# A new order for the opening's list of steps in a fused attention and feed-forward kernel

## Chip, core and metric

The kernel runs on one core of a Trainium2 chip. The metric is the time of one execution on the device, in microseconds (us). The engines of the core work side by side: TensorE (PE in the profile, its weight loads PEld), VectorE (DVE), ScalarE (ACT), GpSimd (POOL) and SyncE (SP). GpSimd and SyncE also issue transfers between the chip's memory and the core's on-chip memory; one queue belongs to each.

## What is computed

Sliding-window causal attention (window 64, sequence 576, 8 batches of 8 heads of 64), whose output feeds a two-layer block with the activation h * cos(h):

```python
scores = (1 / sqrt(D)) * q @ k.T                  # per batch and head
mask = (rel >= 0) & (rel < 64)                    # rel = query position - key position
attn = softmax(where(mask, scores, -1e9))
x = (attn @ v) as (8 * 576, 8 * 64)               # 4608 tokens of 512
h = x @ w_in                                      # 512 -> 2048
out = (h * cos(h)) @ w_out                        # 2048 -> 512
```

Inputs and output are float32; the kernel works on bfloat16 copies of them.

## The kernel before

The 4608 tokens go in nine blocks of 512 (mt = 0 to 8). For each block the attention output of the tokens must stand transposed in a tile xT; TensorE then forms h in 16 slices of 128 features (h_ps), ScalarE takes the sine of h plus a quarter turn (that is the cosine), VectorE multiplies both (gT), and TensorE forms the output from gT and w_out.

Attention works on groups of up to four units (a pair of heads and 64 query rows each). A group goes through scores (TensorE), row maximum (VectorE), exponential with its row sum (ScalarE), reciprocal of the sum (VectorE), normalisation (a multiply, GpSimd or VectorE), transposition of the weights (TensorE and a copy, or a transposing transfer of SyncE), and the product with v (TensorE).

Within each engine instructions run in the order of the program text, so that order is the schedule. From block 1 on a planner with due times interleaves attention of a later batch with the feed-forward of the current block. For the opening, which is block 0's attention and feed-forward and block 1's attention, the order is written out by hand in the string FIRST: 300 steps, separated by blanks. A step is a name and its arguments, separated by points; a last letter d, a, p or s gives the engine (VectorE, ScalarE, GpSimd, a transfer of SyncE), a last digit of s, Gs, h and o the PSUM bank (0 to 4 for O1, X0, X1, S, O0). The names:

- Lq, Lk, Lv, Lwi, Lwo: loads of q, k, v and of quarters of w_in and w_out (first argument of Lq, Lk, Lv: the batch). All are issued by GpSimd, except Lq0.0 and Lk0.0 by SyncE, which cq and ck then cast. io, mk, mc: the masks.
- tq, tk, Tq, Tk: transpositions of a pair of heads of batch 0 and 1 on TensorE (line 202), and pq, pk, Pq, Pk: the copies out of PSUM (lines 123, 224, 226).
- s, m, e, i, n, w, c with pair and half: scores (lines 306, 313), maximum (323), exponential (340), reciprocal (350), normalisation (357), transposition (373) and its copy (123) for a group of batch 0. Gs, Gm, Ge, Gi, Gn, Gw or Gc, Gp with a number: the same for groups 8 to 18. Gc of groups 9 to 14 is a transposing transfer of SyncE (376). In Gm (line 328) the masked scores go into one of six tiles.
- zA, zB, zC, yA, yB, y: copies that lay out v once more, shifted by 64 rows (spread_v).
- v and V: products with v for block 0 and 1 (lines 410, 392); x and X: copies of their output into xT.
- h, S, g: half a block's h product (line 424), its sine (430) and the gate product (436). tb and tb2 load the sine's and the exponential's table.
- o: a quarter of the second product for 128 tokens (line 443); oc: its copy out.

Three PSUM buffers (tag "t", pool ps_t) serve all transpositions and most attention outputs:

```python
ps_t = ctx.enter_context(tc.tile_pool(name="ps_t", bufs=3, space=PSUM))
t_ps = ps_t.tile([128, S], BF16, tag="t", name=f"t{name}_ps")
s = att.tile([128, GF, 128], F32, tag="s", name="s", bufs=6)
```

The second of these is in transposed(), the third in g_max(). A new tile waits until the last reader of the buffer that it takes is done.

Of the kernel before, what the change touches and what calls it, by code (L numbers as in the profile page):

```python
# [10 lines left out]
def _safe_warn(msg, *a, **kw):  # L11
# [31 lines left out]


FIRST = (
# [18 lines left out]
)  # L64


# [670 lines left out]
```

## Time and profile before

| | |
|---|---|
| median of 3 runs | 304.21 us (302.83 to 304.63) |
| profiled execution, its own time | 303.25 us |
| its span, first to last instruction | 301.5 us |
| TensorE busy | 291.7 us (97%) |
| VectorE, ScalarE, GpSimd busy | 233.9, 232.1, 209.1 us |
| packets of GpSimd's transfer queue | 100192, 18.06 MB |
| granted TensorE clock | 1.0 |

Times in the profile count from the start of the span. A timeline row has start, duration, engine, line, operation, tiles (out<-in), shapes and count, and in brackets the idle time of the engine before it and what ended that. A row of the groups has a count, the time busy and the mean duration in nanoseconds, then the idle time ahead. A row of the transfers ends with the median time from issue to landing. A row of the chain of work that ended last has start, duration and what.

### The profile page before, as it was taken

How to read it: one execution, taken by the hardware profiler on the slowest of the kernel's cores; microseconds unless marked ns; L12 is line 12 of the kernel's file. 1: busy time of each engine (PE TensorE's matmuls, PEld its weight loads, DVE VectorE, ACT ScalarE, POOL GpSimd, SP SyncE). 2: the span in 40 equal slices, each digit the busy share in tenths (PEclk: the TensorE clock that was granted, in tenths of full speed). 3: DMA queues.
4: the chain of work that ended last, by engine and by line, in shares of the span. 5: the costliest groups of instructions: out<-in, count | busy, mean ns of one | idle time of the engine just before them, and what ended most of it. 6: DMA issues, size and time to landing. Idle time of an engine off the chain costs nothing.

```text
span 301.5 us, 8520 instructions
## 1 busy us (share of the span) xinstructions
PE 291.7 (97%) x2936; PEld 163.8 (54%) x2936; DVE 233.9 (78%) x915; ACT 232.1 (77%) x781; POOL 209.1 (69%) x238
## 2 busy tenths in 40 slices
PE   3989999999999999999999999999999999999996
PEld 2768854644455445444454445445544454785485
DVE  3798887898887886788678865887588658985794
ACT  5899699877987699769986998699978997304610
POOL 8899568996999689986998799878995860000000
PEclk9999999999999999999999999999999999999999
DMA  7999999999999994999999999999699944003013
GB/s 144 176 205 194 197 188 143 96 139 175 222 116 99 234 143 94 100 149 199 181 106 150 186 159 121 128 196 176 120 97 133 203 88 157 0 3 141 1 35 107
DMA packets 158732, 41.47 MB, mean 138 GB/s; under 512 B 146976, under 2 KB 154336, under 8 KB 158688
## 3 DMA queue, kind: packets, MB, share of 16 engines
q0 software_dynamic: 100192, 18.06, 84.0%
q1 hardware_dynamic: 58352, 22.79, 40.8%
q8 instruction: 23, 0.38, 0.5%
q14 instruction: 21, 0.17, 0.2%
q10 hardware_dynamic: 144, 0.07, 0.1%
HBM read 36.70 MB, written 9.44 MB: 153 GB/s over the span
## 4 chain that ended last, share of the span: by engine, by line
PE 80%; DMA 10%; ACT 6%; POOL 1%; issue 1%; DVE 0%; POOLq 0%; SPq 0%
PE h_ps L460 37%; PE out_ps L697 23%; PE out_ps L547 8%; DMA w_out<-in_moe_w_out_dram 6%; ACT e L340 5%; PE out_ps L443 3%; PE o_ps L392 3%; PE s_ps L291 2%; DMA wT<-w 2%; DMA k<-in_k_dram 2%; PE tq_ps L205 1%; PE s_ps L313 1%; POOL w L357 1%; PE s_ps L306 0%; ACT kT L123 0%
## 5 line engine op out<-in xcount | busy, mean ns | idle before, releaser
L460 PE MATMUL h_ps<-xT,w_in 128*128 128x512 bf16 x512 | 115.1, 379 | 0.2
L686 DVE TENSOR_TENSOR gT<-h_ps,sin 128x512 bf16<-128x512 f32 x128 | 85.2, 688 | 25.8 <-ACT sin L683 25.2
L683 ACT ACTIVATE sin<-h_ps 128x512 f32<-128x512 f32 x128 | 73.8, 598 | 37.3 <-PE h_ps L460 37.0
L340 ACT ACTIVATE e<-s,negm 128x128 f32<-128x128 f32 (+1 forms) x256 | 97.1, 381 | 2.0 <-DVE negm L328 1.0
L697 PE MATMUL out_ps<-w_out,gT 128*128 128x512 bf16 x384 | 85.3, 379 | 0.0
L357 POOL TENSOR_TENSOR w<-e,rden 128x512 bf16<-128x512 f32 (+1 forms) x68 | 69.1, 1034 | 17.0 <-DVE rden L350 12.6
L460 PEld LDWEIGHTS <-w_in 128*128 128x128 bf16 x512 | 48.9, 98 | 54.4
L697 PEld LDWEIGHTS <-gT 128*128 128x128 bf16 x384 | 36.5, 98 | 43.1
L328 DVE CUSTOM_DVE_ANT_0 s<-s_ps,mask 128x128 f32<-128x128 f32 (+1 forms) x256 | 56.0, 277 | 2.0 <-PE s_ps L313 1.7
L340 ACT ACTIVATION_READ_ACCUMULATOR e<-s,negm 128x1 f32 x256 | 48.0, 188 | 0.0
L168 POOL DMA_DIRECT2D q<-in_q_dram x36 | 28.6, 794 | 13.5 <-DMA v<-in_v_dram 5.3
L174 POOL DMA_DIRECT2D v<-in_v_dram x40 | 34.2, 869 | 1.1 <-DMA q<-in_q_dram 1.1
L168 POOL DMA_DIRECT2D k<-in_k_dram x36 | 28.5, 792 | 1.3 <-DVE gT L686 0.6
L350 DVE RECIPROCAL rden<-den 128x4 f32<-128x4 f32 (+1 forms) x73 | 12.2, 167 | 18.8 <-ACT e L340 18.5
L123 POOL COPY v<-v 64x1536 bf16<-64x1536 bf16 (+3 forms) x16 | 22.9, 1433 | 0.4
L328 DVE DVE_READ_ACCUMULATOR2_ANT negm<- 128x1 f32 x256 | 21.3, 83 | 0.0
L123 DVE CAST xT<-o_ps 128x512 bf16<-128x512 f32 x24 | 15.6, 680 | 4.9 <-PE o_ps L392 4.7
L443 PE MATMUL out_ps<-w_out,gT 128*128 128x512 bf16 x64 | 14.8, 379 | 0.2 <-DMA w_out<-in_moe_w_out_dram 0.2
L424 PE MATMUL h_ps<-xT,w_in 128*128 128x256 bf16 x128 | 14.7, 273 | 0.0
L547 PEld LDWEIGHTS <-sums 128*128 128x128 bf16 x136 | 12.2, 98 | 2.0 <-DVE sums L492 0.4
L424 PEld LDWEIGHTS <-w_in 128*128 128x128 bf16 x128 | 12.3, 98 | 1.4
L123 ACT CAST xT<-o_ps 128x512 bf16<-128x512 f32 x12 | 7.1, 612 | 6.4 <-PE o_ps L392 6.4
(85 smaller groups left out, 312.4 us busy)
## 6 DMA issues: line engine op xcount, KB each, us to landing
out_dram<-out_sb SPq DMA_DIRECT2D x16, 512.0 KB, 7.7
v<-in_v_dram POOLq DMA_DIRECT2D x32, 128.0 KB, 6.0
q<-in_q_dram POOLq DMA_DIRECT2D x36, 96.0 KB, 8.6
k<-in_k_dram POOLq DMA_DIRECT2D x36, 96.0 KB, 9.0
w_in<-in_moe_w_in_dram POOLq DMA_DIRECT2D x4, 512.0 KB, 9.0
w_out<-in_moe_w_out_dram POOLq DMA_DIRECT2D x4, 512.0 KB, 11.3
q<-in_q_dram POOLq DMA_DIRECT2D x7, 144.0 KB, 6.3
k<-in_k_dram POOLq DMA_DIRECT2D x7, 144.0 KB, 6.2
```

Of the source, the lines that this page charges most:

```text
L123: {"a": nc.scalar.copy, "p": nc.gpsimd.tensor_copy}.get(engine, nc.vector.tensor_copy)(out, in_)
L168: nc.gpsimd.dma_start(out=st[name, b][:, c].rearrange("p (h d) -> p h d", h=H), in_=src.rearrange("h p d -> p h d"))
L174: nc.gpsimd.dma_start(out=vt.rearrange("p (h d) -> p h d", h=H), in_=v[b, :, c * 128:c * 128 + n, :].rearrange("h p d -> p h d"))
L328: nc.vector.tensor_tensor_reduce(out=s[:, u, c], in0=s_ps[:, u, c], in1=mask[:, 2 - j % 2 if j else 0, c], scale=-scale if b else -1.0, sc ...
L340: nc.scalar.activation(e[:, u, c], s[:, u, c], AF.Exp, bias=negm[:, u:u + 1], scale=1.0 if n < n_first else -1.0, accum_out=den[:, u:u + 1])
L357: (nc.gpsimd if engine == "p" else nc.vector).tensor_tensor(out=w[:, 0:u], in0=e[:, 0:u], op=ALU.mult, in1=rden[:, 0:u].unsqueeze(2).to_br ...
L424: nc.tensor.matmul(out=h_ps[:, half * e:half * e + half], lhsT=w_in_sb[:, ks, ff * 128:ff * 128 + 128], rhs=st["xT", 0][:, ks, half * g:ha ...
L460: nc.tensor.matmul(out=st["h", ff], lhsT=w_in_sb[:, ks, ff * 128:ff * 128 + 128], rhs=st["xT", mt][:, ks], start=start, stop=stop)
L547: nc.tensor.matmul(out=to[n_] if split else to[:, e], lhsT=lhs[name][f // 2][:, f % 2, 128 * e:128 * e + 128], rhs=rhs[name][:, f, lo:hi], ...
L683: nc.scalar.activation(sin, h_ps, AF.Sin, bias=math.pi / 2.0)
L686: nc.vector.tensor_tensor(out=gt[:, e], in0=h_ps, in1=sin, op=ALU.mult)
L697: nc.tensor.matmul(out=o_ps[e], lhsT=gT[ff // 2][:, ff % 2, ms * 128:ms * 128 + 128], rhs=w_out_sb[:, ff], start=ff == 0, stop=ff == n_ff - 1)
```

## The change

Only the string FIRST changes. Both lists have 300 steps and issue the same loads, products and copies. 46 steps have another engine or bank: four normalisations (n.3.1, Gn.13, Gn.8, Gn.9) go from GpSimd to VectorE; the copies zB.0 and zC go from SyncE's transfers to GpSimd, zB.1 from there to VectorE, yB from GpSimd to VectorE; some copies out of PSUM change between ScalarE and VectorE (pk.0, pk.1, Pq.0, Pk.0, x.0.0, x.0.1, x.1.1, the three c of the second half, Gp.8, oc.0, X.2, X.3); the remaining differ in their bank alone. Nearly all steps have a new place, among them the loads: the last two of batch 0's v stand behind two quarters of w_in.

```diff
--- before.py
+++ after.py
@@ -43,24 +43,24 @@
 
 
 FIRST = (
-    "io Lq0.0 Lk0.0 mk cq.d mc ck.a tq.0 Lq0.1 pq.0.d Lk0.1 tk.0 pk.0.a s.0.0.0 Lq0.2 tq.1 tk.1 m.0.0 pq.1.a s.0.1.1 "
-    "Lk0.2 tq.2 pk.1.d s.1.0.2 Lq0.3 Lk0.3 tk.2 s.1.1.3 e.0.0 tq.3 m.0.1 Lq1.0 Lk1.0 Lq1.1 pq.2.d pk.2.d Lk1.1 tk.3 "
-    "m.1.0 s.2.0.4 Lv0.0 Lv0.1 Tq.0 Lv0.2 pk.3.d m.2.0 e.0.1 pq.3.a i.0.0 e.1.0 Tk.0 s.3.0.0 Tq.1 e.2.0 Lv0.3 Lwi.0 "
-    "Pq.0.d i.1.0 Lwi.1 m.3.0 m.1.1 i.2.0 Pk.0.a e.3.0 Lwi.2 Tk.1 n.1.0.p s.2.1.1 Pq.1.d Gs.10.2 m.2.1 Gs.9.4 "
-    "n.0.0.p Pk.1.a n.2.0.p i.3.0 e.1.1 w.0.0 zA.0.d w.1.0 c.0.0.d Gs.12.0 w.2.0 n.3.0.p i.0.1 c.1.0.d zA.1.d "
-    "c.2.0.d e.2.1 zB.0.s zB.1.s n.0.1.p i.1.1 w.3.0 v.0.0 c.3.0.d x.0.0.a s.3.1.3 Gm.10 v.1.0 m.3.1 i.2.1 Gs.11.2 "
-    "Gm.9 Gm.12 n.1.1.p x.1.0.a e.3.1 w.0.1 w.1.1 c.1.1.a i.3.1 h.0.0.1 h.0.1.4 tb n.2.1.p c.0.1.d Lwi.3 w.2.1 "
-    "h.0.2.0 n.3.1.p v.0.1 S.0.0 Gm.11 w.3.1 S.0.1 h.0.3.3 Lwo.0 S.0.2 c.2.1.d c.3.1.d v.1.1 zC.s g.0.0 S.0.3 "
-    "h.0.4.2 x.0.1.a x.1.1.d h.0.5.1 g.0.1 h.1.0.4 g.0.2 g.0.3 S.0.4 h.0.6.0 h.1.1.3 S.0.5 S.1.0 Lq1.2 S.0.6 g.0.4 "
-    "S.1.1 g.1.0 h.1.2.2 Lk1.2 Lq1.3 h.0.7.4 g.0.5 h.1.3.1 Lv1.0 Lwo.1 g.1.1 S.1.2 h.1.4.3 g.0.6 Lk1.3 S.0.7 h.1.5.0 "
-    "g.1.2 h.1.6.2 Lwo.2 g.0.7 S.1.3 S.1.4 S.1.5 Lwo.3 h.1.7.4 Lv1.1 S.1.6 g.1.3 g.1.4 S.1.7 g.1.5 Lv1.2 g.1.6 tb2 "
-    "Tk.2 Lv1.3 Pk.2.d Ge.10 Tq.2 Pq.2.d Tq.3 Ge.9 Ge.12 o.0.0.1 Pq.3.d o.1.0 Tk.3 Gs.14.3 Gs.13.0 Pk.3.d Lv0.4 "
-    "Lq2.0 Ge.11 Gi.10 Gm.14 g.1.7 Lq2.1 Lq2.2 o.0.1.2 Gi.9 o.2.0 Ge.14 Gn.10.p Gm.13 Gc.10 Gi.12 o.1.1 Gs.8.3 "
-    "Gs.16.4 Gm.8 o.3.0 Ge.13 o.2.1 Gi.11 oc.0.d Gn.9.p o.3.1 Gs.15.0 Gs.17.1 Gn.12.p o.0.2.3 Gi.14 Gm.15 oc.1.d "
-    "Gc.9 Gn.11.p Gi.13 Gm.16 o.1.2 Ge.8 Ge.16 Ge.15 y.1.d Gn.14.p yA.p Gi.8 Gc.12 Gm.17 o.0.3.0 Gi.16 Gn.13.p yB.p "
-    "Gc.11 Gn.8.p Lq2.3 Lq2.4 Lq2.5 o.2.2 o.3.2 o.1.3 Gn.16.d Gi.15 Gn.15.d Gw.8 Gc.14 Gc.13 Lk2.0 Gp.8.d Gw.16 "
-    "Lk2.1 Ge.17 Lk2.2 Gp.16.d Gi.17 Lk2.3 o.2.3 oc.2.a Gw.15 Gp.15.d V.0 V.1 V.2 V.3 Gs.18.4 X.0.a X.1.d X.2.a "
-    "X.3.d Gm.18 o.3.3 oc.3.d Ge.18 Gn.17.d Lk2.4 Gi.18 Gn.18.d Lk2.5 Lv1.4 "
+    "io Lk0.0 Lk0.1 Lq0.1 Lq0.3 ck.a Lq0.2 Lk0.2 tk.0 mk Lk1.1 Lq0.0 cq.d mc Lq1.0 pk.0.d Lk0.3 tq.0 tk.1 Lq1.1 "
+    "pq.0.d pk.1.a tq.1 s.0.0.4 pq.1.a m.0.0 s.0.1.3 s.1.0.1 tq.2 Lv0.1 Lk1.0 Lv0.0 m.1.0 tk.2 e.0.0 m.0.1 pq.2.d "
+    "e.1.0 tq.3 s.1.1.0 i.0.0 pk.2.d m.1.1 s.2.0.4 Lwi.0 Lwi.1 m.2.0 Lv0.2 s.2.1.2 Lv0.3 tk.3 Tq.0 pk.3.d i.1.0 "
+    "pq.3.a e.0.1 s.3.0.3 e.2.0 n.0.0.p Tq.1 s.3.1.1 Pq.0.a Tk.0 n.1.0.p i.0.1 m.2.1 m.3.0 Tk.1 e.3.0 i.2.0 "
+    "zA.0.d Pk.0.d n.2.0.p Pq.1.d Pk.1.a e.1.1 i.3.0 Lwi.2 Gs.9.4 w.0.0 w.1.0 n.3.0.p Gs.11.3 e.2.1 n.0.1.p "
+    "zA.1.d c.0.0.d c.1.0.d Gm.9 w.2.0 v.0.0 w.3.0 c.2.0.d i.1.1 c.3.0.d x.0.0.d m.3.1 i.2.1 Gm.11 n.1.1.p "
+    "Gs.12.0 v.1.0 Lq1.3 x.1.0.a Gs.10.4 e.3.1 w.0.1 h.0.1.2 Gm.12 tb w.1.1 h.0.2.3 c.1.1.d i.3.1 S.0.1 Lwi.3 "
+    "n.2.1.p w.2.1 zB.1.d n.3.1.d g.0.1 Lwo.1 zB.0.p Lq2.1 Lq1.2 Lwo.0 Lk1.2 Lk1.3 zC.p h.0.3.0 c.2.1.a c.0.1.a "
+    "Lq2.2 w.3.1 c.3.1.d h.0.0.1 v.0.1 v.1.1 S.0.3 S.0.2 x.1.1.a S.0.0 Gm.10 x.0.1.d g.0.2 g.0.3 h.0.4.2 h.1.0.4 "
+    "h.1.2.0 g.0.0 h.0.5.1 S.0.4 g.0.4 S.0.5 S.1.0 h.1.1.2 h.0.6.3 g.0.5 g.1.0 S.1.1 S.0.6 h.0.7.1 h.1.5.4 g.0.6 "
+    "h.1.4.3 g.1.1 S.1.2 S.0.7 S.1.4 g.1.2 h.1.6.2 h.1.3.0 g.0.7 g.1.4 S.1.6 S.1.3 Lq2.0 h.1.7.3 Tq.2 Lv1.1 Lwo.2 "
+    "Tq.3 Tk.2 Lwo.3 g.1.6 g.1.3 Pq.2.d S.1.7 S.1.5 o.0.1.1 g.1.7 Pk.2.d tb2 o.0.0.2 Ge.10 Gs.14.3 Gs.13.0 Lv1.3 "
+    "Tk.3 Pq.3.d Lv1.0 g.1.5 Ge.12 o.1.1 o.0.3.4 o.1.3 Gi.10 Gm.13 Gm.14 Ge.13 Ge.11 Gn.10.p Pk.3.d Gi.12 Gn.12.p "
+    "Gs.16.0 Gs.8.3 Gm.8 o.1.0 Gm.16 Gi.13 o.2.1 Gs.15.3 Gs.17.0 Ge.8 Ge.9 Ge.14 Gi.11 Gn.13.d Gm.15 Gm.17 Gi.8 "
+    "Gn.8.d Gi.9 Ge.15 Lv1.2 Ge.16 Ge.17 Lq2.4 Gn.11.p o.3.1 o.0.2.3 o.2.0 Gn.9.d yB.d o.1.2 Gw.8 o.2.3 o.2.2 "
+    "o.3.0 o.3.2 Gi.14 Gn.14.p Lv0.4 yA.p oc.1.d y.1.d Gi.15 Gn.15.d Gi.16 Lq2.5 Lk2.2 Lq2.3 Lk2.0 Lk2.1 Gp.8.a "
+    "Lk2.3 Gc.10 oc.2.a Gi.17 Gw.15 o.3.3 Gn.16.d Gw.16 Lk2.4 Lk2.5 Gc.12 Gn.17.d Gc.13 Gc.11 Gs.18.3 oc.0.a Gc.9 "
+    "Gp.15.d Gp.16.d V.0 X.0.a V.3 V.1 Gc.14 X.3.a Gm.18 V.2 X.1.d Ge.18 X.2.d Lv1.4 oc.3.d Gi.18 Gn.18.d "
 )
```

## The prediction

> **What bounds the kernel now.** I read the busy times by stage first, then the timelines of TensorE, ScalarE, VectorE and GpSimd for the first 60 us, then groups of instructions by shape for durations. The stages are cut where the first `h` product starts (21.91), where its long unbroken run starts and ends (26.84, 37.42), and where the second token block begins (57.04).
>
> ```profile
> core 0: us, PE busy (x) PEld busy (x) DVE busy (x) ACT busy (x) POOL busy (x), PEclk, DMA share, GB/s
> 0.00:21.91 21.91, 15.63 (x386) 12.42 (x387) 15.22 (x44) 16.84 (x70) 18.69 (x32) 1.00 1.24 173
> 21.91:26.84 4.93, 4.93 (x76) 4.06 (x73) 3.87 (x25) 4.90 (x15) 4.73 (x7) 1.00 1.20 218
> 26.84:37.42 10.58, 10.58 (x101) 9.31 (x97) 9.07 (x15) 7.65 (x14) 7.41 (x10) 1.00 1.30 188
> 37.42:57.04 19.62, 19.43 (x265) 10.71 (x265) 16.31 (x81) 17.73 (x79) 15.46 (x19) 1.00 1.54 147
> 57.04:90.00 32.96, 32.93 (x302) 16.49 (x301) 28.50 (x122) 28.27 (x102) 28.07 (x33) 1.00 1.93 160
> ```
>
> TensorE idles 21.91 - 15.63 = 6.28 us before the first `h` product and 0.2 us from there to 57.04, so from 21.91 on every delay of TensorE's queue moves the end, and nothing later gives it back (0.03 us idle in the last row). Only before 21.91 do other engines decide. What decides there, in the timelines of TensorE, VectorE and ScalarE (start, duration, instruction, idle time before it):
>
> ```profile
> 4.15 0.69 PE L202 MATMUL tq_ps<-ident,q 64*64 64x64 bf16 x18 [4.15 <-DVE q L123]
> 7.75 0.69 PE L202 MATMUL tk_ps<-ident,k 64*64 64x64 bf16 x18 [0.23 <-DMA k<-in_k_dram]
> 8.26 0.61 PE L306 MATMUL s_ps<-mask,ident 64*64 64x512 bf16 x2
> 8.66 0.63 PE L313 MATMUL s_ps<-kT,qT 64*64 64x128 bf16 x8
> 9.09 0.68 PE L202 MATMUL tq_ps<-ident,q 64*64 64x64 bf16 x18
> 14.26 0.38 PE L306 MATMUL s_ps<-mask,ident 64*64 64x512 bf16 x2
> 14.48 0.36 PE L313 MATMUL s_ps<-kT,qT 64*64 64x64 bf16 x8
> 14.68 0.45 PE L202 MATMUL tq_ps<-ident,q 64*64 64x64 bf16 x18
> 26.84 10.65 PE L424 MATMUL h_ps<-xT,w_in 128*128 128x256 bf16 x96
> 56.88 2.75 PE L460 MATMUL h_ps<-xT,w_in 128*128 128x512 bf16 x12
> 59.47 0.42 PE L205 MATMUL tq_ps<-ident,q 96*128 96x96 bf16 x6
> ```
> ```profile
> 7.08 0.69 DVE L323 TENSOR_REDUCE negm<-s_ps 128x4 f32<-128x512 f32 x1 [1.45 <-PE s_ps L313]
> ```
> ```profile
> 25.43 2.04 ACT L430 ACTIVATE sin<-h_ps 128x512 f32<-128x512 f32 x4
> ```
>
> The first row maximum starts at 7.08; eight rounds of maximum (VectorE) and exponential (ScalarE) follow, and the first sine at 25.43 stands behind all eight.
>
> **The change part by part.** The 300 steps are the same work. 46 have another engine or bank, and nearly all another place. I step through the new list by hand: a step starts at the latest of its engine, its data and its buffer. Durations, from the groups by shape in the first 57 us and from the chain that ended last:
>
> ```profile
> L123 DVE COPY kT<-tk_ps 128x576 bf16<-128x576 bf16 x5 | 3.8, 758 | 2.3 <-PE tk_ps L202 2.3
> L123 ACT COPY kT<-tk_ps 128x576 bf16<-128x576 bf16 x3 | 2.0, 681 | 0.8 <-PE tk_ps L202 0.8
> L323 DVE TENSOR_REDUCE negm<-s_ps 128x4 f32<-128x512 f32 x8 | 5.4, 683 | 1.5 <-PE s_ps L313 1.4
> L328 DVE CUSTOM_DVE_ANT_0 s<-s_ps,mask 128x128 f32<-128x128 f32 x35 | 8.1, 284 | 0.4 <-PE s_ps L313 0.4
> L436 DVE TENSOR_TENSOR gT<-h_ps,sin 128x512 bf16<-128x512 f32 x16 | 10.4, 686 | 1.4 <-ACT sin L430 1.3
> L357 POOL TENSOR_TENSOR w<-e,rden 128x512 bf16<-128x512 f32 x12 | 12.4, 1045 | 2.1 <-DVE rden L350 2.1
> L357 DVE TENSOR_TENSOR w<-e,rden 128x512 bf16<-128x512 f32 x1 | 0.7, 692 | 0.0
> L123 POOL COPY v<-v 64x1024 bf16<-64x1024 bf16 x1 | 1.0, 1031 | 0.0
> L340 ACT ACTIVATE e<-s,negm 128x128 f32<-128x128 f32 x33 | 12.7, 386 | 1.0 <-DVE negm L328 1.0
> L455 ACT ACT_TABLE_LOAD x1 | 1.3, 1283 | 0.0
> ```
> ```profile
> 18.35 2.81 ACT e L340 x16
> 2.49 5.22 DMA k<-in_k_dram
> ```
>
> One exponential group is 2.81 / 2 = 1.40 us.
>
> *Engines.* Four normalisations (n.3.1, Gn.13, Gn.8, Gn.9) leave GpSimd (4 x 1.045 = 4.2 us) for VectorE (4 x 0.692 = 2.8). The copies of `v` leave SyncE's transfers for GpSimd (zB.0, zC: 1.03 each) and VectorE (zB.1). x.0.0 and c.1.1 leave ScalarE before the sines, a relief of about 1.2 us there. Alone these edits cost TensorE nothing: the copies have until v.0.1, and GpSimd is under the other engines' pace.
>
> *Start.* k's rows now come first, and TensorE's order is tk.0, tq.0, tk.1, tq.1, **then** s.0.0. tk.1 and tq.1 need the first two transfers of GpSimd's queue:
>
> ```profile
> q<-in_q_dram POOLq DMA_DIRECT2D x1, 144.0 KB, 4.6
> ```
> ```profile
> 1.75 0.74 POOL L151 DMA_DIRECT2D q<-in_q_dram  x1
> ```
>
> They land at 1.75 + 4.6 = 6.3 and 2.49 + 5.22 = 7.71. So tk.1 runs at 6.4, tq.1 at 7.75, and s.0.0 only at 8.25; 0.5 us of tq.1 stand before it, its masks and products take 0.83 (8.26 to 9.09) and end 0.2 later, so the first maximum starts at 9.32 instead of 7.08: **+2.24 us**.
>
> *From there to the first `h` product.* VectorE sets the pace: m.1.0 11.0 (its scores wait for pq.1 and tq.1), pk.2 13.7, m.2.0 14.4, pk.3 15.8, m.3.0 16.5, Pk.0 18.3, Pq.1 19.0 (w.0.0 takes the PSUM buffer it frees), c.0.0 and c.1.0 20.1, Gm.9 20.9, c.3.0 21.6, x.0.0 22.2. On ScalarE e.2.1 ends at 21.8 (eight rounds fit behind 10.0, with the relief), x.1.0 at 22.75. The first product, h.0.1, starts at 22.8 instead of 21.91, with one transposition (w.1.1, 0.2) still owed: **+1.1**. About half of the late start is won back, since x.0.0 runs on VectorE meanwhile.
>
> *The wait at w.3.1.* Three PSUM buffers serve transposes and attention outputs. That they are taken in turn, I read from three rows:
>
> ```profile
> 12.43 0.65 ACT L224 ACTIVATE qT<-tq_ps 128x576 bf16<-128x576 bf16 x1 [0.86 <-PE tq_ps L202]
> ```
> ```profile
> 12.91 0.76 DVE L123 COPY kT<-tk_ps 128x576 bf16<-128x576 bf16 x1 [0.46 <-PE tk_ps L202]
> ```
> ```profile
> 13.49 0.35 PE L202 MATMUL tk_ps<-ident,k 64*64 64x64 bf16 x11
> ```
>
> Tk.0 starts at 13.49, before the copy of tk.3 (listed earlier than pq.3) ends at 13.67, so it took the buffer of tq.3, free at 13.08: the oldest in turn. In the new list w.3.1 then takes w.0.1's buffer, freed by c.0.1, which now is on ScalarE behind the table load, S.0.1 and c.2.1. e.3.1 waits for m.3.1 (VectorE, 22.8) and ends at 24.2; load 1.28 and its first use bring S.0.1 to 25.63, c.2.1 to 26.15, c.0.1 to 27.1. TensorE has finished h.0.3 at 26.1 (the stretch from 21.91 to 26.84 holds four products, two transpositions and two rounds of attention output; I use its pace) and stands **1.0 us**, with h.0.0, v.0.1, v.1.1 and h.0.4 queued behind. 1.1 + 1.0: h.0.4 starts at about 29.0 instead of 26.84, **+2.1**.
>
> *The rest of `h`.* VectorE's 0.62 to 0.69 per gate and TensorE's 10.65 / 12 = 0.89 per product keep the same order as before; banks come free at most 0.1 us late. It ends at about 39.4 instead of 37.42: **+2.0**. The weights are hidden:
>
> ```profile
> w_in<-in_moe_w_in_dram POOLq DMA_DIRECT2D x4, 512.0 KB, 9.0
> ```
>
> w_in's third quarter is issued at 18.3 (behind n.2.0), so 27.3 against h.0.4 at 29.0; its fourth at 22.9, so 31.9 against h.0.6 at 33. w_out, issued from 24.7, has only three chunks of q and one of v more ahead of its last quarter, and is not needed before 40.
>
> *Second part.* Scores Gs.16 wait 0.15 for Pk.3, which stands behind Gm.13 and Gm.14 on VectorE. Gm.8 writes the seventh of six score tiles. The buffer in turn, Gm.9's, is still in use (Ge.9 is listed later), so the next, Gm.11's, is the likely one, free only when Ge.11 ends at 47.4; Gs.8 is there at 46.5. VectorE stands 0.9, and Gm.16, Gn.13, Gm.15 queue behind; TensorE waits 0.5 at Gs.17 for its bank (Gm.16) and 0.5 at o.0.2 (Gm.15). At the end Gp.16, behind Gi.17, Gn.16, Gn.17 and Gp.15 on VectorE, costs V.3 about 0.2, inside the above. 0.15 + 0.5 + 0.5: **+1.1**, and the second block's first product (56.88) starts at about 60.0: 2.0 + 1.1 = **+3.1**.
>
> The four moved normalisations sit in that last piece: three of them, 2.1 us of VectorE, between 48 and 53. Their cover is ScalarE's exponentials, 36 units of 0.386 from 42 to 56.8, Gm.8's wait included; without it they would cost up to 2.1. Bounds of unknown sizes: the copy zB.1 costs VectorE between nothing and the 1.03 that GpSimd takes for that size, I take 0.55, nearer VectorE's 0.76 for a larger tile; and the transposed weights' flight is unknown here between nothing and the 5.22 of the k chunk: at that end Gc.14, issued about 53.8, lands at 59.0, before V.2 wants it (59.6). Nothing is charged for either.
>
> [...] Masks and products of a score group take 0.42 us from start to start at 14.26 (to 14.68) and 0.83 at 8.26 (to 9.09): TensorE works at half speed at first, though the clock column shows 1.00. [...]
>
> [...]
>
> ```profile
> 51.35 1.03 POOL L357 TENSOR_TENSOR w<-e,rden 128x512 bf16<-128x512 f32 x1
> ```
> ```profile
> 52.06 0.73 DVE L357 TENSOR_TENSOR w<-e,rden 128x384 bf16<-128x384 f32 x1
> ```
>
> 384 elements took 0.73 on VectorE beside GpSimd's multiply until 52.38, and 512 took 0.69 alone. [...]
>
> **The sum.** The profiled execution took 303.25 (span 301.5). With +3.1 it is 306.35. The median of the runs shown is 304.21, 0.96 above; so I forecast **307.3**.
>
> **The rivals.**
>
> 1. *Gm.8's tile comes without a wait* (the allocator hands out the one released first, Gm.10's, at 43.2): 0.9 less, 306.4. For: the trace never shows a turn being skipped. Against: the rows at 13.49 show turns, not release order.
> 2. *Neither buffer waits*: c.0.1's 1.0 goes, since n.3.1 ends at 26.1, and Gm.8's 0.9: 1.9 less, 305.4. Against: the same rows.
> [...]
>
> ```profile
> q<-in_q_dram POOLq DMA_DIRECT2D x2, 96.0 KB, 3.9
> ```
>
> 4. *It gets faster.* The relief on ScalarE decides, if the loads for tk.1 and tq.1 land by 5.5 and tq.1 has ended by 6.1: s.0.0 would then reach the first maximum at 7.08 as before, the eight exponentials and x.1.0 end 1.2 earlier, and TensorE fills that much of its 6.28 idle. Price -1.2 with c.0.1 no longer waited for: 303.0. Against: 6.3 and 7.71.
>
> **How the numbers follow.** Forecast 0.45, rivals 0.20, 0.08, 0.20, 0.07. What a measurement tells from no change is about 1%, 3.04 us: slower begins at 307.25. Of the forecast's own spread (306.2 to 308.5, leaning up since waits add) two thirds, 0.30, lie above; of rival 1 0.03; rival 3 all 0.20: slower 0.53. Faster by 1% needs 301.2, beyond rival 4's price but within its miss: 0.05. Same 0.42. The range for 8 in 10 takes rival 2 at its lower side and rival 3 with a second such wait: 303.9 to 310.6; rival 4 is left out.
>
> **What would show it.** First maximum at about 9.3; first `h` product at 22.8; TensorE idle 1.0 us ahead of w.3.1 near 26, released by ScalarE's c.0.1; the unbroken `h` run ending at 39.4; Gm.8 released by Ge.11; the second block starting at 60.0, its stages after that as long as now. A first maximum near 7, or a TensorE gap near 26 under 0.3, makes the forecast wrong; a second block at 57 makes it worthless, and one past 62 shows a wait that I missed.

## The result and the profile after

The changed kernel took 304.85 us in the median (303.54 to 305.71), the kernel before 303.6 (302.28 to 304.91), 22 runs each: a ratio of 1.0039 with a 95% interval of 1.0024 to 1.0054, or **+1.2 us**. That is slower, and less than the 1% that the prediction counts as a difference. The forecast was +3.1 us; sign and range hold, the size does not. The profiled execution took 304.79 us by its own time, with a span of 302.9 (before: 303.25 and 301.5).

The busy times by stage, cut at the same four events as before: first `h` product (22.03), begin and end of the unbroken `h` run (27.64, 38.38), second token block (58.03; its first product starts at 57.87, as 56.88 goes with the prediction's 57.04).

```profile
core 0: us, PE busy (x) PEld busy (x) DVE busy (x) ACT busy (x) POOL busy (x), PEclk, DMA share, GB/s
0.00:22.03 22.03, 15.22 (x382) 11.83 (x383) 15.07 (x43) 16.39 (x68) 18.60 (x32) 1.00 1.25 175
22.03:27.64 5.61, 5.46 (x79) 4.23 (x77) 5.19 (x29) 5.28 (x16) 5.60 (x7) 1.00 1.20 177
27.64:38.38 10.74, 10.74 (x103) 9.22 (x98) 8.34 (x16) 6.72 (x13) 8.19 (x12) 1.00 1.44 178
38.38:58.03 19.65, 19.55 (x265) 10.44 (x265) 18.60 (x85) 18.44 (x81) 10.85 (x14) 1.00 1.16 132
58.03:91.00 32.97, 32.94 (x302) 16.37 (x301) 28.47 (x119) 28.51 (x103) 28.18 (x34) 1.00 1.93 163
```

The four stages take 0.12, 0.68, 0.16 and 0.03 us more than before (22.03 against 21.91, 5.61 against 4.93, 10.74 against 10.58, 19.65 against 19.62), and the long last one the same pace. So the loss of 1.0 at the second block has its largest piece in 5 us around 25, where the forecast put 1.2 (the wait of 1.0 and the 0.2 of the transposition w.1.1), and next to nothing in the second part, where it put 1.1. TensorE's timeline through that place:

```profile
6.65 0.69 PE L202 MATMUL tk_ps<-ident,k 64*64 64x64 bf16 x18 [0.99 <-DMA k<-in_k_dram]
7.46 0.69 PE L202 MATMUL tq_ps<-ident,q 64*64 64x64 bf16 x18
7.96 0.61 PE L306 MATMUL s_ps<-mask,ident 64*64 64x512 bf16 x2
...
22.03 1.04 PE L424 MATMUL h_ps<-xT,w_in 128*128 128x256 bf16 x8
22.90 0.39 PE L373 MATMUL tw_ps<-ident,w 128*128 128x128 bf16 x4
23.29 1.03 PE L424 MATMUL h_ps<-xT,w_in 128*128 128x256 bf16 x8
24.43 0.40 PE L373 MATMUL tw_ps<-ident,w 128*128 128x128 bf16 x4
24.67 1.04 PE L424 MATMUL h_ps<-xT,w_in 128*128 128x256 bf16 x8
25.73 0.40 PE L373 MATMUL tw_ps<-ident,w 128*128 128x128 bf16 x4
25.97 1.04 PE L424 MATMUL h_ps<-xT,w_in 128*128 128x256 bf16 x8
27.01 0.69 PE L410 MATMUL o_ps<-wT,v 128*64 128x64 bf16 x32
...
57.87 2.79 PE L460 MATMUL h_ps<-xT,w_in 128*128 128x512 bf16 x12
```

Read it start to start. A product needs 0.87 (22.03 to 22.90), a transposition 0.24 (24.43 to 24.67). A start that comes later than that is a gap: h.0.2 at 23.29 stands 0.15 late, w.2.1 at 24.43 stands 0.27, w.3.1 at 25.73 stands 0.19 and v.0.1 at 27.01 stands 0.17. No bracket marks these gaps, since the row of a product lasts 1.04, longer than the 0.87 to the next start. Each start follows the end of one row on another engine (VectorE, GpSimd, VectorE, ScalarE):

```profile
22.95 0.28 DVE L328 CUSTOM_DVE_ANT_0 s<-s_ps,mask 128x128 f32<-128x128 f32 x1
...
24.98 0.69 DVE L357 TENSOR_TENSOR w<-e,rden 128x512 bf16<-128x512 f32 x1
```
```profile
23.32 1.06 POOL L357 TENSOR_TENSOR w<-e,rden 128x512 bf16<-128x512 f32 x1
```
```profile
24.02 1.28 ACT L455 ACT_TABLE_LOAD   x1
...
25.90 1.06 ACT L123 COPY wT<-tw_ps 128x512 bf16<-128x512 bf16 x2
```

Gm.11 frees the bank of h.0.2 at 23.23; n.2.1 ends at 24.38, n.3.1 at 25.67, c.0.1 at 26.96. Four gaps make 0.78. One transposition (w.1.1) that the kernel before did ahead of the first product adds 0.23. Before had about 0.2 of such gaps in its stage, and the two attention products stand together now, which saves 0.12: 0.78 + 0.23 - 0.2 - 0.12 = 0.69, the stage's 0.68 within rounding.

### The profile page after: what moved, and what is told of

The parts are those of the page before. It is cut to its first block, busy times and chain, and to the rows that moved or that the text cites. A ratio compares the mean times of both kernels' runs of the same rounds, so it can differ in the third digit from the quotient of the medians.

```text
span 302.9 us, 8502 instructions
## 1 busy us (share of the span) xinstructions
PE 292.1 (96%) x2936; PEld 163.0 (54%) x2936; DVE 236.6 (78%) x919; ACT 232.1 (77%) x783; POOL 206.2 (68%) x235
## 4 chain that ended last, share of the span: by engine, by line
PE 83%; DVE 7%; DMA 4%; ACT 2%; POOL 2%; issue 1%; POOLq 0%; SPq 0%; DVEq 0%
PE h_ps L460 37%; PE out_ps L697 23%; PE out_ps L547 8%; PE h_ps L424 4%; PE o_ps L392 2%; PE s_ps L291 2%; DMA wT<-w 2%; ACT e L340 2%; PE out_ps L443 2%; DMA q<-in_q_dram 2%; PE tq_ps L205 1%; DVE s L328 1%; DVE negm L323 1%; POOL w L357 1%; DVE w L357 1%
## 5 line engine op out<-in xcount | busy, mean ns | idle before, releaser
L686 DVE TENSOR_TENSOR gT<-h_ps,sin 128x512 bf16<-128x512 f32 x128 | 85.0, 688 | 25.6 <-ACT sin L683 25.0
L357 POOL TENSOR_TENSOR w<-e,rden 128x512 bf16<-128x512 f32 (+1 forms) x64 | 65.2, 1033 | 24.9 <-DVE rden L350 15.3
L123 POOL COPY v<-v 64x1024 bf16<-64x1024 bf16 (+3 forms) x17 | 23.8, 1398 | 0.5
L436 DVE TENSOR_TENSOR gT<-h_ps,sin 128x512 bf16<-128x512 f32 x16 | 10.4, 685 | 2.8 <-ACT sin L430 2.6
```

Of the source, the lines that this page charges most:

```text
L123: {"a": nc.scalar.copy, "p": nc.gpsimd.tensor_copy}.get(engine, nc.vector.tensor_copy)(out, in_)
L357: (nc.gpsimd if engine == "p" else nc.vector).tensor_tensor(out=w[:, 0:u], in0=e[:, 0:u], op=ALU.mult, in1=rden[:, 0:u].unsqueeze(2).to_br ...
L686: nc.vector.tensor_tensor(out=gt[:, e], in0=h_ps, in1=sin, op=ALU.mult)
```

## The experiments

The theories, by the letters of the expectations. A: the loss is made between 22 and 28 us, where TensorE waits for late normalisations of the second half and for a bank. B: the late start keeps everything late. C: VectorE's extra work in the second part is the loss, three of the four moved normalisations among it. D: ScalarE's unbroken string from the first exponential to c.0.1 sets the pace. N: normalisations on VectorE are a gain wherever they stand. All versions were timed beside the kernel before, 6 to 12 runs each; the kernel before had medians of 303.04 to 303.72 there, so compare ratios and not medians. "Run" is the start of the unbroken `h` run, "block 2" that of the second block, in the single profiled execution. The first maximum of one and the same opening lies between 8.57 and 9.50 (in e1, f2 and after tk.1 waits for its chunk until 6.40, 6.55 and 6.65, and the maximum starts at 8.73, 8.79 and 8.99), so half a microsecond of one profile decides nothing; stretches between two events of a profile are steadier. The step of TensorE to full speed, described at the end, moves the opening of a single profile too: e1 and f2 start the same masks at 7.70 and 7.76, and a later pair, with the same steps between, at 10.78 and 11.66.

| label | median us | ratio to before, 95% | first maximum | run | block 2 |
|---|---|---|---|---|---|
| before | 303.6 | 1 | 7.08 | 26.84 | 56.88 |
| after | 304.85 | 1.0039 (1.0024 to 1.0054) | 8.99 | 27.64 | 57.87 |
| e1_norms | 309.09 | 1.018 (1.0135 to 1.0225) | 8.73 | 27.61 | 62.18 |
| e2_start | 304.54 | 1.0026 (1.0005 to 1.0046) | 7.22 | 26.91 | 57.15 |
| e3_weights | 304.67 | 1.0037 (1.0016 to 1.0059) | 9.50 | 28.14 | 58.37 |
| e4_first_of_before | 303.46 | 0.999 (0.9968 to 1.0012) | 7.33 | 27.88 | 57.68 |
| e5_c_vector | 305.35 | 1.0052 (1.003 to 1.0074) | 8.84 | broken, 29.64 | 59.72 |
| e6_before_norms | 310.06 | 1.0214 (1.0178 to 1.0249) | 7.18 | 26.68 | 62.86 |
| e7_v_first | 303.8 | 1.0008 (0.998 to 1.0035) | 8.57 | 27.05 | 57.01 |
| e8_all | 304.66 | 1.005 (1.0024 to 1.0076) | 7.25 | broken, 30.08 | 58.72 |
| f1_start_v | 303.56 | 1.0007 (0.9987 to 1.0027) | 7.21 | 27.53 | 57.49 |
| f2_buffer_wait | 305.12 | 1.0065 (1.0047 to 1.0083) | 8.79 | 28.15 | 58.28 |
| f3_loads_late | 303.93 | 1.0032 (1.0011 to 1.0053) | 7.16 | 26.89 | 57.63 |
| f4_scalar_relief | 303.8 | 1.0021 (1.0 to 1.0042) | 7.10 | 27.35 | 57.27 |
| g1_v_behind_win | 311.74 | 1.0274 (1.0238 to 1.031) | 7.03 | 33.31 | 63.32 |
| g2_start_of_after | 306.2 to 312.79 | none | 8.81 | 29.76 | 59.57 |
| g3_middle_of_after | 305.92 | 1.0085 (1.0052 to 1.0117) | 7.02 | 29.70 | 59.56 |

**Which part?** e4_first_of_before: before's list up to tb2 (the end of the `h` part), then after's remaining steps.

```diff
- after's steps up to the end of the h products
+ before's steps up to tb2
  after's remaining steps
```

> The list of before up to the end of the h products (to tb2), then the changed list's remaining steps in their order. Theories A and B: the loss is made ahead of that cut, so the second block starts at 56.9 to 57.1 and the time is that of before. Theory C: the second part loses what it loses in the changed kernel, 57.9.

0.999: no loss is left that can be measured. It takes the first part of the new order to make it, and the second part alone costs nothing. From the start of the run to block 2 it is 29.80 us here, 30.04 in before and 30.23 in after, so a little of what the first part does shows only later. (The profile has its own late run, a wait of 1.01 for a sine ahead of v.0.1. At 304.56 it is the longest of the 12 timed runs, so this is not the usual course.)

**The start.** e2_start: the first scores and maximum ahead of tk.1.

```diff
-tq.0 tk.1 Lq1.1 pq.0.d pk.1.a tq.1 s.0.0.4 pq.1.a m.0.0
+tq.0 pq.0.d s.0.0.4 m.0.0 tk.1 Lq1.1 pk.1.a tq.1 pq.1.a
```

> The changed kernel with pq.0, s.0.0 and m.0.0 ahead of tk.1, so that the first scores no longer stand behind tk.1 and tq.1 on TensorE. First maximum at about 7.3 instead of 8.99 and the first exponential about 0.8 earlier (behind pq.1). Theory A: the first h product was only 0.1 late, so the second block starts at 57.6 to 57.9. Theory B: 0.8 earlier on every engine, 57.0 to 57.2. Theory C: 57.9.

The first maximum starts 1.77 earlier, but the first exponential only 0.72 (9.00 against 9.72), since pk.1 and pq.1 still stand ahead of it on ScalarE, and the run 0.73. That profile, at 303.39, is the shortest of the 12 timed runs. The median improves by 0.13%, inside both intervals. So the late start is not shown to cost anything, and f1 below agrees.

**Late normalisations.** e3_weights: n.2.1 ahead of the loads on GpSimd, n.3.1 ahead of the copy zB.1 on VectorE.

```diff
-n.1.1.p Gs.12.0 v.1.0 Lq1.3 ... Lwi.3 n.2.1.p w.2.1 zB.1.d n.3.1.d
+n.1.1.p n.2.1.p Gs.12.0 v.1.0 Lq1.3 ... Lwi.3 w.2.1 n.3.1.d zB.1.d
```

> The changed kernel with n.2.1 ahead of the loads Lq1.3 and Lwi.3 in GpSimd's order, and n.3.1 ahead of the copy zB.1 in VectorE's. Theory A: n.2.1 ends at 23.5 instead of 24.4 and n.3.1 at 25.0 instead of 25.7; TensorE's waits ahead of w.2.1 (0.27) and w.3.1 (0.19) go, and the second block starts at 57.4. Theory B: the exponentials are as late as before this edit, 57.8 or later. Theory C: 57.9.

Nothing gained, 1.0037. The gaps ahead of w.2.1 and w.3.1 went, and v.0.1 then stood 0.31 for ScalarE's c.0.1: from the first exponential to v.0.1 it is 17.29 us here and in after (10.22 to 27.51, 9.72 to 27.01). Taking one wait away uncovers the next.

**Relief of ScalarE.** e5_c_vector moves c.0.1 to VectorE and the late normalisations forward, and puts the gate g.0.1 behind c.3.1; e8_all does this with the early start and zB.1 on GpSimd; f4_scalar_relief takes x.0.0 and c.1.1 off ScalarE in e4's list.

```diff
 e5: -c.0.1.a            +c.0.1.d (behind n.3.1.d, ahead of zB.1.d), n.2.1.p and zB.0.p earlier, g.0.1 behind c.3.1.d
 e8: as e5, but c.0.1.d ahead of c.1.1.d; +pq.0.d s.0.0.4 m.0.0 tk.1, Lwi.3 behind n.2.1.p, zB.0.p zB.1.p Lq1.3 behind w.2.1
 f4: -x.0.0.a c.1.1.a    +x.0.0.d c.1.1.d
```

> The changed kernel with c.0.1 on VectorE instead of ScalarE behind S.0.1 and c.2.1; so that nothing else takes its place, n.2.1 and zB.0 go ahead of Lq1.3 on GpSimd, n.3.1 and c.0.1 ahead of zB.1 and c.3.1 ahead of g.0.1 on VectorE. Theory D (ScalarE works without a break from the first exponential to c.0.1, 17.2 us, and v.0.1 waits for it): v.0.1 starts 17.3 to 17.5 us after the first maximum instead of 18.0, and the second block 0.5 earlier than in the changed kernel for the same first maximum, 57.3. Theory A (only the two late normalisations): as the third run, which moved those alone, no gain. Theory B (the start alone counts): no gain for the same first maximum.

> The changed kernel with the earlier start of the second run (pq.0, s.0.0, m.0.0 ahead of tk.1), c.0.1 on VectorE, n.2.1 and n.3.1 early, zB.1 on GpSimd like zB.0, and Lwi.3 ahead of both copies. Theory D: first maximum 7.2, h.0.4 at 26.4 (26.84 before, 27.64 in the changed kernel), second block at 56.4 to 56.6: 0.1 to 0.2% below the kernel before. Theory B alone: as the second run, 57.1. Rival: a late quarter of w_in or w_out (their loads go 1 to 2 us later) takes the gain, 57 or later.

> Before's list up to tb2 and after's remaining steps (alone 0.999), with x.0.0 and c.1.1 moved from ScalarE to VectorE in the first part. Theory (ScalarE's string from the first exponential to the first copies and sines sets when the unbroken run of h products starts): 1.1 us less on ScalarE before its table load, so h.0.4 starts 0.5 to 1.0 earlier than without the edit and the time is 302.6 to 303.1, ratio 0.996 to 0.998. Rival (VectorE is as full there, and the two copies push its maxima, gates and weights back by as much): h.0.4 no earlier, 303.5 or more, ratio 0.999 to 1.004.

Theory D missed in all three; in f4 the rival's time came (303.8, 1.0021). In e5's timeline of TensorE the run is broken by VectorE, and later by a load:

```profile
27.21 1.03 PE L424 MATMUL h_ps<-xT,w_in 128*128 128x256 bf16 x8 [0.22 <-DVE gT L436]
28.44 1.03 PE L424 MATMUL h_ps<-xT,w_in 128*128 128x256 bf16 x8 [0.20 <-DVE xT L123]
29.64 9.20 PE L424 MATMUL h_ps<-xT,w_in 128*128 128x256 bf16 x80 [0.17 <-DVE gT L436]
40.80 0.47 PE L202 MATMUL tk_ps<-ident,k 64*64 64x64 bf16 x18 [1.27 <-DMA k<-in_k_dram]
```

e8 waits 0.60 at w.3.1 for VectorE, and in f4 the run starts behind a quarter of w_in:

```profile
27.35 10.65 PE L424 MATMUL h_ps<-xT,w_in 128*128 128x256 bf16 x96 [0.42 <-DMA w_in<-in_moe_w_in_dram]
```

In the kernel after VectorE is as full as ScalarE here (5.19 and 5.28 busy of 5.61), so work moved from one to the other can come back as a wait on the other. e5 and e8 do not show that cleanly: the first of e5's waits is for g.0.1, which the same edit put behind c.3.1. My theory that ScalarE's string alone sets the run found no support.

**The buffer wait that was forecast.** f2_buffer_wait exchanges the engines of c.1.1 and c.2.1, so that the only buffers released ahead of w.3.1 are ScalarE's.

```diff
-c.1.1.d i.3.1 ... h.0.3.0 c.2.1.a c.0.1.a Lq2.2 w.3.1 c.3.1.d
+i.3.1 ... h.0.3.0 c.1.1.a c.0.1.a Lq2.2 w.3.1 c.2.1.d c.3.1.d
```

> The kernel after, with the copies c.1.1 and c.2.1 exchanged: c.1.1 on ScalarE behind the first sine, c.2.1 on VectorE listed behind w.3.1. ScalarE and VectorE do as many copies as before this edit, but the only buffers that are released ahead of w.3.1 in the list are now released by ScalarE, which is the wait that the prediction charged. Theory (the step was right in its price and wrong in which buffer is taken): w.3.1 starts when ScalarE's first copy ends, about 26.4 instead of 25.73, the idle time ahead of it is 0.7 and released by ScalarE, h.0.4 starts at about 28.3 and the second block 0.7 later: 305.5 us, ratio 1.006. Rival: the wait is paid out of the wait for c.0.1 at v.0.1 and costs nothing, 304.85, ratio 1.004.

```profile
26.33 0.38 PE L373 MATMUL tw_ps<-ident,w 128*128 128x128 bf16 x4 [0.83 <-ACT wT L123]
```

The wait appears, 0.83 long and released by ScalarE, and the ratio goes from 1.0039 to 1.0065, +0.8 us. The two intervals just overlap and block 2 is only 0.41 later in the profile, so the size is rough. w.3.1 starts when ScalarE's first copy is done, half a microsecond before the second one, c.0.1, is. So the step's price and the chain behind it were about right. In the kernel after it was the wrong buffer.

**The normalisations.** e1_norms gives the four back to GpSimd in after's list; e6_before_norms moves them to VectorE in before's; f3_loads_late is e6 with Gn.16 given back to GpSimd ahead of batch 2's loads.

```diff
 e1: after,  -n.3.1.d Gn.13.d Gn.8.d Gn.9.d  +n.3.1.p Gn.13.p Gn.8.p Gn.9.p
 e6: before, -n.3.1.p Gn.13.p Gn.8.p Gn.9.p  +n.3.1.d Gn.13.d Gn.8.d Gn.9.d
 f3: e6,     -Lq2.3 Lq2.4 Lq2.5 ... Gn.16.d  +Gn.16.p Lq2.3 Lq2.4 Lq2.5
```

> The changed kernel with its four moved normalisations (n.3.1, Gn.13, Gn.8, Gn.9) back on GpSimd at their new places. Measure: the start of the second block's first product, 56.88 us before and 57.87 in the changed kernel. Theory A (the loss is made between 22 and 28 us, where TensorE waits for the last two normalisations of block 0 and a bank): n.3.1 starts on GpSimd at 24.4 right behind n.2.1 and ends about 25.4, 0.25 earlier than on VectorE, but the copy zB.0 behind it ends about 27.6 and holds v.0.1 (27.01) by 0.6: 58.0 to 58.4. Theory B (the late first maximum keeps everything late): 57.9. Theory C (VectorE's extra work in the second part is the loss): 57.0 to 57.4.

> The kernel before with the four normalisations on VectorE and nothing else changed. Theory D and A: off the path there, where GpSimd gives n.3.1 in time; the same time within 0.3%, second block at 56.9 plus or minus 0.3. Theory N (normalisations on VectorE are a gain wherever they stand, as putting them back cost 4.3 us in the changed kernel): a second block at 56.5 or earlier. Rival to both: VectorE has 3.3 us idle of 19.6 in that part, and 2.1 us more there delay a bank or a gate by up to 1 us: 57.5 to 57.9.

> The kernel before with four normalisations on VectorE (alone 1.0214), and Gn.16 given back to GpSimd with batch 2's loads of q and k behind it. Theory (the loss of 6 us there is a collision: a relieved GpSimd issues those ten loads from 49.3 instead of 52.3, and the last transposing transfers of the weights then take 7.4 us instead of 2.5): with Gn.16 ahead of the loads they are issued from about 52 to 53, the last transposed weights land near 55, V does not wait for them, and the time is 304 to 305, ratio 1.00 to 1.005. Rival: the loss comes from the normalisations on VectorE themselves (the transfers start late because Gn.9 ends late on VectorE): then most of it stays, 308 to 310, ratio 1.015 or more.

Opposite edits both cost: e1 4.2 us over the kernel after, e6 6.3 over the kernel before. In e1 the waiting normalisations hold back Lv1.2 behind them in GpSimd's order (issued at 50.78 instead of 45.94), VectorE stands for that load, and TensorE for VectorE:

```profile
54.70 1.82 DVE L123 COPY v<-v 64x2048 bf16<-64x2048 bf16 x1 [3.49 <-DMA v<-in_v_dram]
```
```profile
58.01 0.61 PE L373 MATMUL tw_ps<-ident,w 128*128 128x128 bf16 x4 [3.24 <-DVE w L357]
```

In e6 the relieved GpSimd issues batch 2's loads from 49.3 instead of 52.3, between SyncE's transposing transfers. The last two of these take 7.4 and 7.6 us from issue to landing (before: 3.3 and 2.5), the last landing at 59.63. The transfers from 42 to 58 and TensorE's wait:

```profile
k<-in_k_dram POOLq DMA_DIRECT2D x6, 96.0 KB, 7.5
q<-in_q_dram POOLq DMA_DIRECT2D x4, 96.0 KB, 6.4
wT<-w SPq DMA_TRANSPOSE x6, 5.2
```
```profile
59.67 1.01 PE L392 MATMUL o_ps<-wT,v 128*64 128x64 bf16 x30 [4.62 <-DMA wT<-w]
```

f3 gives Gn.16 back to GpSimd and its loads leave at 52.8. The last two transposing transfers take 2.9 and 3.6 us, and the same views show the wait gone:

```profile
k<-in_k_dram POOLq DMA_DIRECT2D x4, 96.0 KB, 3.7
q<-in_q_dram POOLq DMA_DIRECT2D x3, 96.0 KB, 3.4
wT<-w SPq DMA_TRANSPOSE x6, 3.5
```
```profile
55.05 1.43 PE L392 MATMUL o_ps<-wT,v 128*64 128x64 bf16 x64
```

1.0214 becomes 1.0032: nearly all of the loss was a collision of transfers, not VectorE's time for the multiplies.

**The loads of v.** e7_v_first puts Lv0.2 and Lv0.3 ahead of w_in in the kernel after, f1_start_v adds e2's start, and g1_v_behind_win puts them behind two quarters of w_in in the kernel before.

```diff
 e7: after,  -Lwi.0 Lwi.1 m.2.0 Lv0.2 s.2.1.2 Lv0.3   +Lv0.2 Lv0.3 Lwi.0 Lwi.1 m.2.0 s.2.1.2
 g1: before, -Lv0.2 ... Lv0.3 Lwi.0 Pq.0.d i.1.0 Lwi.1 +Lwi.0 Pq.0.d i.1.0 Lwi.1 Lv0.2 Lv0.3
```

> The changed kernel with the last two loads of batch 0's v (Lv0.2, Lv0.3) ahead of the first two quarters of w_in again. All theories so far: no difference, the products h.0.1 and h.0.2 have their quarters 2 us early even if these land 1.7 us later; second block as in the changed kernel for the same first maximum. Rival: h.0.2 waits for its quarter, up to 0.5 us later.

> The kernel after, with the two edits that gained anything alone: pq.0, s.0.0 and m.0.0 ahead of tk.1 (alone 1.0026 of the kernel before, against 1.0039 for the kernel after), and the last two loads of v ahead of w_in (alone 1.0008). Theory: the two act at different places (ScalarE's string up to c.0.1, and Gw.15's copy near 54 us), so they add up: h.0.4 starts about 0.7 earlier than in the kernel after, the second block about 1.0 earlier, 303.3 to 303.7 us, ratio 0.997 to 1.001. Rival: the gain of the loads was noise of that comparison, then the time is that of the early start alone, 304.5, ratio 1.0026. For a version faster than before by more than the uncertainty the ratio would have to be under 0.998; I give that one chance in four.

> The kernel before with one piece of the change: the last two loads of v (batch 0) behind the first two quarters of w_in, in GpSimd's queue. Theory V (these two loads carry the loss: with them ahead of w_in the kernel after came to 1.0008 and 1.0007 instead of 1.0039): the copies that lay out v for the second half start later, and the time is 304.2 to 304.6, ratio 1.003. Rival (the loads have until the second products with v at 25, and those comparisons differed by their uncertainty): nothing changes, ratio 1.000 with at most 0.002 either way, first h product at 21.9 and unbroken run at 26.8 as before.

e7 and f1 come to 1.0008 and 1.0007, two comparisons that agree and whose intervals contain no change; f1's early first maximum adds nothing (its run starts at 27.53). The traces show 0.27 of this gain, in the stretch from the run to block 2 (29.96 in both, 30.23 in after, e2 30.24, e3 30.23). It does not sit where v is used for block 0. In after, e2 and e3 GpSimd's multiply Gn.14 starts 24.08 or 24.09 behind the start of the run and lies beside VectorE's copy y.1, in e7 and f1 it starts at 23.72, and y.1 is shorter; TensorE's Gw.15, which stands behind both, follows 0.27 earlier (27.13 against 27.40). Why Gn.14 is earlier there is not shown. The copy in after and in f1:

```profile
51.83 1.27 DVE L123 COPY v<-v 64x2048 bf16<-64x2048 bf16 x1
```
```profile
51.71 0.91 DVE L123 COPY v<-v 64x2048 bf16<-64x2048 bf16 x1
```

Neither is faster than before.

g1 missed by 7 us, and shows the most. Its chain of work that ended last, from 10 to 35 us (start, duration, what):

```profile
12.63 10.05 DMA v<-in_v_dram
...
22.76 6.05 DMA v<-v
28.81 1.11 issue
29.92 0.64 PE o_ps L410 x16
```

The last chunk of v lands at 22.68 instead of 17.45. In the kernel before zB is a transfer of SyncE, 6.05 long, so v.0.1 waits until 29.92 and the run starts 6.47 later, at 33.31. In the kernel after the same loads land at 22.30 and 23.14, and the copies follow on VectorE in 0.63 (24.32) and on GpSimd in 1.30 (25.26): no wait. The late loads and the new engines of the copies, two parts of the change, belong together: **the late loads alone cost 8.4 us, and the copies by GpSimd and VectorE bear them.** The second half is read from the trace of after; no run changes the copies alone.

**Ahead of w.0.1 or behind it?** g2_start_of_after is after's list up to w.0.1, then before's; g3_middle_of_after the other way round.

```diff
 g2: +after up to e.3.1, then before's remaining steps up to tb2, then after's
 g3: +before up to e.3.1, then after's remaining steps
```

> After's steps up to the end of the first half (everything ahead of w.0.1: start, loads, engines of the copies), then before's order up to tb2, then after's. Theory S (the start and the first half carry the loss): the first maximum is at 8.6 to 9.0, the first h product at about 22.5, the unbroken run at 27.4 to 27.7, ratio 1.003 to 1.004. Theory M (the order from w.0.1 to the unbroken run carries it, because w.1.1 stands behind an h product and three transpositions or products wait for other engines): the run starts at about 27.0, ratio 0.999 to 1.001.

> Before's steps up to the end of the first half (ahead of w.0.1), then after's order. Theory S: the first maximum is at 7.1 to 7.4, the first h product at 21.8 and the unbroken run at 26.8, ratio 0.999 to 1.001. Theory M: the first h product starts about 0.2 earlier than before (one transposition less ahead of it), but the waits ahead of w.2.1, w.3.1 and v.0.1 come back and the run starts at 27.3 to 27.6, ratio 1.002 to 1.004.

Neither answers. g3's first product waits 2.10 us for VectorE (23.19 instead of 22), g2's 1.58 for an exponential (23.86), both because the bank that the following list names is still being read in the list ahead of it. g2's six times lie between 306.2 us (the profiled one) and 312.79, so no ratio is given. Each half is fitted to the banks of its own other half.

## Why the prediction was wrong

- **Start**, +2.24 forecast, +1.91 measured (8.99 against 7.08). Right in mechanism: tk.1 waits for its chunk (6.65), tq.1 follows (7.46), s.0.0 at 7.96.
- **From there to the first product**, +1.1 forecast (0.9 at the first product and 0.2 for w.1.1, owed behind it), +0.35 measured (0.12 and 0.23). Mis-sized: "about half won back" was most of it. I stepped VectorE with busy durations, but a maximum of 0.68 lets the next instruction start after 0.60:

```profile
21.12 0.68 DVE L123 CAST xT<-o_ps 128x512 bf16<-128x512 f32 x1
21.72 0.68 DVE L323 TENSOR_REDUCE negm<-s_ps 128x4 f32<-128x512 f32 x1
22.32 0.17 DVE L350 RECIPROCAL rden<-den 128x4 f32<-128x4 f32 x1
```

  From m.1.0 to x.0.0 I had 11.2 (11.0 to 22.2); it took 10.47 (10.65 to 21.12), and the profile marks no idle time of VectorE in between. The trace of before showed the same overlap (a maximum of 0.69 at 9.34, the next instruction at 9.95).
- **The wait at w.3.1**, +1.0 forecast, absent: this is the step that failed. "Three PSUM buffers ... taken in turn" is wrong. w.3.1 starts at 25.73, when n.3.1 ends (25.67), and does not wait for c.0.1 (26.96); its instructions wait for counts of VectorE and TensorE and for none of ScalarE. In the built kernel it lies in the PSUM bank of w.1.1, whose reader c.1.1 ran on VectorE and was done at 24.21. So a tile can take a buffer that was freed earlier than the one whose turn it is, and the three rows at 12.43 to 13.49 fitted that too. f2 shows the wait where all earlier readers are ScalarE's.
- **The rest of h**: nothing of its own forecast, +0.16 measured (10.74 against 10.58), with no cause shown.
- **Second part**, +1.1 forecast, +0.03 measured. Gm.8 started when its scores were there, with no wait for Ge.11, whose last exponential, by the order of ScalarE's list, ended at 46.27 (Gm.8's first row, then that exponential):

```profile
45.27 0.29 DVE L328 CUSTOM_DVE_ANT_0 s<-s_ps,mask 128x128 f32<-128x128 f32 x1 [0.60 <-PE s_ps L313]
```
```profile
45.88 0.39 ACT L340 ACTIVATE e<-s,negm 128x128 f32<-128x128 f32 x1
```

  It is the same wrong rule. Rival 1 named the tile: Gm.8 lies in Gm.10's, the one released first. Rival 2 (neither buffer waits, 305.4, +1.2) had both waits right. Its price matches the measured +1.2 partly by chance: it kept the +1.1 of the piece above, of which 0.35 came, and knew nothing of the gaps of 0.1 to 0.3 behind the first product, which did.
- **The four normalisations**: three of them stand in the second part, which alone costs nothing that can be measured (e4), as said; n.3.1 shows as the 0.19 ahead of w.3.1. That they would cost "up to 2.1" without their cover was too mild: e1 and e6 show 4 and 6, by way of the transfers.
- **The number of steps** with another engine or bank is 48 by the two lists, not 46; nothing hangs on it.
- **Rival 3** held 0.20 of the chances and set the upper end of the range (310.6), and no run shows the time that it added. What the runs showed in its place: a pair of masks is slow at 11.86 (0.61) and nearly at full rate at 12.69 (0.43), as late as in before (0.48 at 12.68); Gn.13 on VectorE (46.98, 0.69) and Gn.11 on GpSimd (47.67, 1.05) ran one behind the other; and the first transposition of the second block came at 60.50 with no idle time ahead of it.

What stays open: how the 1.2 us divide. The late start and the late normalisations, each taken away alone, give back at most 0.13%; ScalarE's copy c.0.1 was moved only together with other steps, and at no gain. The earlier v loads give back 0.3%, about 0.9 us, of which the traces show 0.27 us near 54. g2 and g3 could not split the part, and no version tried beats the kernel before.

## What to carry to other kernels

Step a schedule by hand with start-to-start times, not busy durations, and read which buffer a tile takes from the waits of the compiled instructions; a rule guessed from three rows put 2 of 3 forecast microseconds in the wrong place. Where several engines are all nearly full, a wait removed can uncover the next one (0.31 us in e3), so test a suspected cause by forcing it (f2) as well as by removing it. Before moving a load, name what stands between its landing and its use: a copy of 0.6 to 1.3 us on an engine bears a load that is 5 us later, and a transfer of 6 us does not.

## What the runs showed of the hardware

The step of TensorE to full speed does not come at a fixed time. A transposition of a pair of heads takes 0.69 us at first and 0.45 later. In the kernel after it was still slow at 11.38; in f1, with its first transposition at 4.38 (after: 4.47), fast from 10.04:

```profile
11.38 0.66 PE L202 MATMUL tq_ps<-ident,q 64*64 64x64 bf16 x18
```
```profile
10.04 0.45 PE L202 MATMUL tk_ps<-ident,k 64*64 64x64 bf16 x18
```

Over the sixteen traces here that have a clock record, with the first transposition between 4.1 and 4.5, it lies between 9.5 (g3) and 12.9 (before): in e1 a pair of masks takes 0.56 at 9.33 and a score product 0.36 at 9.73, in before a transposition 0.67 at 12.20 and 0.44 at 13.20. The kernel after stayed slow through 5.2 us in which TensorE had no idle time, from 7.46 to 12.69.

In four versions TensorE lost that speed again around a wait. The mean granted clock was 0.50 from 27.0 to 33.7 us in g1 (TensorE idle 5.21), from 59.7 to 63.0 in e6 (4.62), from 57.5 to 60.8 in e1 (3.24) and from 23.2 to 26.5 in g3 (2.10); over the whole profiled execution it was 0.989 in g1 and 0.994 in the other three, and 1.0 in before, after and g2, which was idle for 1.58. In g1 a product took 1.92 us there (30.89) instead of 1.04; in e1 four matmuls of the second product took 1.91 (58.41) instead of 1.03, in e6 three took 1.49 (61.58) instead of the 0.81 in f3 (56.98). So part of what these four versions lost is half speed behind the wait and not the wait itself.

VectorE took longer beside GpSimd. In the kernel after a multiply of 512 takes 0.69 alone (50.25), and 1.45 where it starts while GpSimd copies (53.38 to 54.43):

```profile
53.53 1.45 DVE L357 TENSOR_TENSOR w<-e,rden 128x512 bf16<-128x512 f32 x1
```
```profile
53.38 1.05 POOL L123 COPY v<-v 64x1024 bf16<-64x1024 bf16 x1
```
